# Seven half-size products for the output in four more chunks of two batches, with the output products a chunk later and the scores placed by slot

## The chip, the cores and the metric

The kernel runs on one core of a Trainium2 chip. The metric is the time on the device in microseconds (us), the median of three runs. TensorE (PE) multiplies matrices into PSUM, VectorE (DVE) and ScalarE (ACT) work on tiles elementwise, GpSimd (POOL) and SyncE (SP) mostly issue transfers here.

## The reference

Four batches of 5,824 tokens with 256 channels go through a channel attention, and then all tokens through a feed-forward network without a nonlinearity but one elementwise product.

```python
B, N, C = (4, 5824, 256);  d_ff = 1024

qn = q / (norm(q, axis=1) + 1e-06)        # norms over the tokens
kn = k / (norm(k, axis=1) + 1e-06)
s = kn.transpose(0, 2, 1) @ qn / tau      # 256 x 256 per batch
a = softmax(s, axis=-1)
x = (v @ a).reshape(B * N, C)

ab  = (x @ w1) * (x @ w2)                 # tokens x 1024
out = (ab @ w3) @ w_out                   # tokens x 256
```

The kernel multiplies `w3 @ w_out` once (`W_sb`, 1024 x 256) and folds the 256 x 256 attention matrix of each batch into `w1` and `w2` (`Wf`). What is left for each token is two products with `Wf`, one elementwise product and one product with `W_sb`.

## The kernel before

A batch has `NCH` = 12 chunks of tokens: 11 of 512 and a last one of 192. A chunk has `FT` = 8 **slots**, one for each 128 of the 1,024 features. A slot computes the tiles `a` and `b` on TensorE, copies `a` to SBUF on ScalarE, and multiplies the two on VectorE into `ab` (`abh` in the profile). The products of `ab` with `W_sb` are put on a list (`pend`) and come some slots later. The batches are b = 0 to 3 in the code; the text counts them as first to fourth.

```python
LAG = 2
def bank(tag):                                 # PSUM
    if tag == "out":
        return {"tag": "out", "bufs": 3}
    turns[0] += 1
    return {"tag": f"ab{turns[0] % 4}", "bufs": 1}

def emit_ab(b, c, j):
    n = chunk_cols(c)                          # 512, in the last chunk 192
    tiles = []
    for w in range(2):
        t = psum.tile([P, 512], F32, name=f"{'ab'[w]}_{b}_{c}_{j}", **bank("ab"))
        for ct in range(CT):                   # two matmuls each
            nc.tensor.matmul(
                t[:, :n], lhsT=Wf[b][:, ct, w, j * P : (j + 1) * P], rhs=rhs_of(b, c, ct),
                start=(ct == 0), stop=(ct == CT - 1),
            )
        tiles.append(t)
    a_sb = work.tile([P, 512], BF16, tag="a_sb", name=f"as_{b}_{c}_{j}", bufs=4)
    nc.scalar.copy(a_sb[:, :n], tiles[0][:, :n])
    # ... (last chunk: into "left")
        if j % 4 == 0:
            halves[j // 4] = in_pool.tile([P, 4, 512], BF16, tag="big", name=f"abh_{b}_{c}_{j}", bufs=BIG_BUFS)
        ab = halves[j // 4][:, j % 4, :]
        nc.vector.tensor_mul(ab, a_sb, tiles[1])
    slot[0] += 1
    if not seven(b, c):
        pend.append((slot[0] + LAG, 1, lambda only=None: emit_out(b, c, j, ab, only)))
    elif j == FT - 1:
        fns = seven_products(b, c, *halves)
        fns[0]()
        pend.extend((slot[0] + 1, 2, fn) for fn in fns[1:])
```

The **direct** way to the output, `emit_out`, makes four matmuls of 256 columns per slot, 32 per chunk, and copies the sums out at the end of the chunk:

```python
def emit_out(b, c, j, ab, only=None):
    # ...
        nc.tensor.matmul(
            tl[h][:, o, :], lhsT=lhsT, rhs=W_sb[:, j, :],           # 256 columns
            start=(j == 0 and o == 0), stop=(j == FT - 1 and (small or o == 1)), skip_group_check=True,
        )
    if j == FT - 1:
        # ...
            nc.scalar.copy(o[:, 0:2, :], tl[0])
            nc.vector.tensor_copy(o[:, 2:4, :], tl[1])
            nc.sync.dma_start(out=rows[:, 4 * c : 4 * c + 4, :], in_=o)
```

The **seven-product** way splits the product of a chunk, `ab` by `W_sb`, into blocks of two by two, and makes seven block products in place of eight, each of eight matmuls of 128 columns (56 per chunk). Sums of blocks of `ab` are made on VectorE, sums of blocks of `W_sb` once (`combine_weights`, in the second batch).

```python
def seven(b, c):
    return b == B - 1 and c < NCH - 2          # ten chunks of the fourth batch

    # in seven_products:
    def keep(r, d):  nc.scalar.copy(quarter(r, d), st["A"])
    def join(nm, r, d):  nc.vector.tensor_add(quarter(r, d), st[nm], quarter(r, d))
    def sum1():  nc.vector.tensor_add(s1, a21, a22)
    def p1():    nc.vector.tensor_sub(s2, s1, a11); product("A", a11, w1, True); keep(0, 0)   # o_sb taken here
    def p5():    nc.vector.tensor_sub(s3, a11, a21); product("C", s1, t1, True)
    def p6():    product("A", s2, t2); keep(0, 1)
    def p7():    nc.vector.tensor_sub(s4, a12, s2); product("A", s3, t3); keep(1, 1)
    def p2():    join("C", 1, 1); product("B", a12, w21, True)
    def p4():    join("B", 0, 0); product("A", a22, t4); keep(1, 0)
    def p3():    product("C", s4, w22); join("C", 0, 1)     # then the transfer out
    return [sum1, p1, p5, p6, p7, p2, p4, p3]
```

While batch b runs, the **scores** of batch b + 1 are made: 23 pairs of token rows, each in three units (`sq` of q with two matmuls, `sq` of k with two matmuls, and the sum of the squares on VectorE). They, the loads (`moves`) and what follows the scores stand on an agenda that runs by a clock, which adds up the kernel's own estimate of the TensorE time:

```python
    # score_units: one pair
    nc.scalar.activation(out=dst[:, :, part, :], in_=src[:, o : o + 2, :], func=AF.Square)   # parts 0, 1
    for ct in range(CT):
        nc.tensor.matmul(G[:, ct, :], lhsT=qt[:, i, ct * P : (ct + 1) * P], rhs=kt[:, i, :], ...)
    nc.vector.tensor_add(accs[n], accs[n], sqs[0])                                           # part 2

    # make_agenda, batches after the first
    t0, t1 = 16.0, 98.0
    for i, (cst, fn) in enumerate(units):
        at(t0 + (t1 - t0) * i / len(units), cst, fn)
    for cst, t, fn in soft:                    # norms, exponentials, folding into Wf
        at(t1 + 1.0 + t, cst, fn)

for b in range(B):
    make_agenda(b)
    for c in range(NCH):
        for j in range(FT):
            run_due()
            emit_ab(b, c, j)
            # ... up to size 2 of what is due on pend, run_due() after each
```

Of the kernel before, what the change touches and what calls it, by code (L numbers as in the profile page):

```python
# [17 lines left out]
LAG = 2  # L18
# [7 lines left out]
def kernel(  # L26
# [14 lines left out]
    B, N, C = q.shape  # L41
# [9 lines left out]
    FT = F // P  # L51
# [414 lines left out]
    comb = {}  # L466

    def seven(b, c):
        return b == B - 1 and c < NCH - 2

    def combine_weights(step):

# [100 lines left out]
    def emit_ab(b, c, j):  # L573
        n = chunk_cols(c)
# [11 lines that stand above are left out]
        if c == NCH - 1:  # L586
            if b % 2 == 0 and j == 0:
                lefts[b // 2] = work.tile([P, FT, 2, P + LEFT], BF16, tag="left", name=f"left_{b}", bufs=1)
            both = lefts[b // 2][:, j, b % 2, :]
            nc.vector.tensor_mul(both, a_sb[:, :n], tiles[1][:, :n])  # L590
            ab = both[:, :P] if b % 2 == 0 else both[:, LEFT:]
        else:
# [4 lines that stand above are left out]
        last_ab[0] = ab  # L597
        slot[0] += 1
        if not seven(b, c):
            pend.append((slot[0] + LAG, 1, lambda only=None: emit_out(b, c, j, ab, only)))  # L600
        elif j == FT - 1:
            fns = seven_products(b, c, *halves)
            fns[0]()
            pend.extend((slot[0] + 1, 2, fn) for fn in fns[1:])
        clock[0] += 4 * (n * MM_COL + MM_FIX)

    def emit_out(b, c, j, ab, only=None):

        small = c == NCH - 1
        if small:  # L610
            lhs = [ab[:, :P]]
            if b % 2 == 1:
                lhs.append(lefts[b // 2][:, j, :, :].rearrange("p b t -> p (b t)")[:, P : P + 2 * LEFT])
        else:
            lhs = [ab[:, i * P : (i + 1) * P] for i in range(4)]
        if j == 0:
            out_tiles[b, c] = [
                psum.tile([P, 2, D], F32, tag="out", name=f"o_{b}_{c}_{h}", bufs=3)
                for h in range(len(lhs) if small else 2)
            ]  # L620
        tl = out_tiles[b, c]
        for s, lhsT in reversed(list(enumerate(lhs))) if small else enumerate(lhs):
            if only is not None and s != only:
                continue
            h, o = (s, 0) if small else divmod(s, 2)
            nc.tensor.matmul(  # L626
                tl[h][:, o, :], lhsT=lhsT, rhs=W_sb[:, j, :],
                start=(j == 0 and o == 0), stop=(j == FT - 1 and (small or o == 1)),
                skip_group_check=True,
            )  # L630
        clock[0] += len(lhs) * (D * MM_COL + MM_FIX)
        if j == FT - 1:
            o = work.tile([P, 4, D], F32, tag="o_sb", name=f"osb_{b}_{c}", bufs=3)
            rows = out[b * N : b * N + NT * P, :].rearrange("(p i) c -> p i c", i=NT)
            if small:
                if b % 2 == 1 and only != 0:
                    o2 = work.tile([P, D], F32, tag="kr", name=f"oleft_{b}", bufs=1)
                    nc.vector.tensor_copy(o2, tl[1][:, 0, :])
                    for m in (b - 1, b):
                        k = (m - b + 1) * LEFT  # L640
                        nc.sync.dma_start(out=out[m * N + NT * P : (m + 1) * N, :], in_=o2[k : k + LEFT, :])
                if only != 1:
                    nc.scalar.copy(o[:, 0, :], tl[0][:, 0, :])
                    other = nc.scalar if b == B - 1 else nc.sync
                    other.dma_start(out=rows[:, NT - 1, :], in_=o[:, 0, :])
            else:
# [3 lines that stand above are left out]
            if only is None:  # L650
                del out_tiles[b, c]
# [114 lines left out]
        nc.gpsimd.partition_all_reduce(m, ones_f, P, ReduceOp.add)  # L766


    def make_agenda(b):
        agenda.clear()  # L770
        clock[0] = 0.0
        n = b + 1
        if b == 0:
            at(0.5, 0.87, soft0[5])
            for i in range(4):
                at((1.7, 2.6, 3.5, 3.9)[i], 0.43, soft0[7 + i])
            at(0.0, 0.0, load_library)
            at(4.6, 0.5, lambda: transpose_half_on_pe(0, 0, 1, False))
            at(7.0, 0.5, lambda: transpose_half_on_pe(0, 1, 0, True))
            at(8.0, 0.5, lambda: transpose_half_on_pe(0, 1, 1, False))  # L780
            at(15.0, 0.0, transpose_w3)
            at(15.0, 0.0, lambda: transpose_piece(0, 2))
            for jt in range(FT):
                at(27.5 + 1.2 * jt, 0.87, lambda jt=jt: w_unit(jt))
            moves = [("qk", 1, 0, 29.0), ("v", 0, 3, 30.0), ("v", 0, 4, 30.5), ("qk", 1, 1, 44.0), ("qk", 1, 2, 45.0)]
            moves += [("qk", 1, 3, 53.0), ("qk", 1, 4, 55.0), ("v", 0, 5, 61.0), ("qk", 1, 5, 73.0)]
            moves += [("v", 1, 0, 88.0), ("v", 1, 1, 98.0), ("v", 1, 2, 120.0), ("qk", 2, 0, 130.0)]
            t0, t1 = 54.0, 113.0
        else:
            moves = [("v", b, 3, 1.0), ("qk", n, 1, 10.0), ("qk", n, 2, 17.0), ("v", b, 4, 26.0), ("qk", n, 3, 38.0)]  # L790
            moves += [("v", b, 5, 46.0), ("qk", n, 4, 58.0), ("qk", n, 5, 66.0)]
            moves += [("v", n, 0, 76.0), ("v", n, 1, 86.0), ("v", n, 2, 96.0), ("qk", n + 1, 0, 108.0)]
            moves = [m for m in moves if m[1] < B]
            t0, t1 = 16.0, 98.0

        before = (0, 2) if b == 0 else None
        for nm, m, pi, t in moves:
            if before is not None and not (nm == "v" and before == (m, pi - 1) == (0, 3)):
                at(t, 0.0, lambda w=before: hold(vTs[w[0]][1][:1, 0, :1] if w[1] == NP_ - 1 else vTs[w[0]][0][:1, w[1] * PIECE, 0, :1]))
            at(t, 0.0, gate)  # L800
            if nm == "qk":
                at(t, 0.0, lambda m=m, pi=pi: load_qk(m, pi))
                before = None
            else:
                at(t, 0.0, lambda m=m, pi=pi: load_piece("v", m, pi))
                at(t + 4.0, 0.0, lambda m=m, pi=pi: transpose_piece(m, pi))
                before = (m, pi)
        if b == 1:
            for i in range(4):
                at(3.0 + 2.6 * i, 0.0, lambda i=i: combine_weights(i))  # L810
        if n == B:
            agenda.sort()
            return
        units = score_units(n)
        for i, (cst, fn) in enumerate(units):
            at(t0 + (t1 - t0) * i / len(units), cst, fn)
        soft = soft_units(n)
        for cst, t, fn in soft:
            at(t1 + 1.0 + t, cst, fn)
        agenda.sort()  # L820

    for b in range(B):
        make_agenda(b)
        for c in range(NCH):
            for j in range(FT):
                run_due()
                emit_ab(b, c, j)
                lag = 0
                if b == B - 1 and c >= NCH - 2:
                    lag = LAG_END if c == NCH - 1 else LAG + (LAG_END - LAG) * (j + 1) // FT  # L830
                room = 2
                while w_ready[0] and len(pend) > lag and pend[0][0] <= slot[0] and pend[0][1] <= room:
                    _, size, fn = pend.pop(0)
                    fn()
                    room -= size
                    run_due()
        run_due(1e9)
# [39 lines left out]
```

## Time and profile before

| | before |
|---|---|
| median of three runs | 566.84 us (566.59 to 566.93) |
| span of the profiled run | 564.8 us |
| granted TensorE clock | 1.0 |
| busy: DVE, ACT, POOL | 403.5 (71%), 348.7 (62%), 78.3 us (14%) |
| weight loads on TensorE (PEld) | 355.3 us (63%) |
| DMA packets | 77.50 MB, mean 137 GB/s |

The profile is of one execution. It lists busy time by engine, the chain of work that ended last, groups of instructions by source line (L579 are the products `a` and `b`, L626 the direct output products, L510 the seven products, L201 the score products, L596 the elementwise product, L585 the copy of `a`, L198 the squares, L210 the sum of squares), and the time of every instruction. For each stretch of the span the busy time of each engine can be read. Weight loads overlap the matmuls.

### The profile page before, as it was taken

The numbers are of one execution on the slowest core, as the hardware profiler recorded it, in microseconds if no ns is written. First come the engines' busy times: TensorE is split into PE (matmuls) and PEld (weight loads), VectorE is DVE, ScalarE is ACT, GpSimd is POOL, SyncE is SP. The second block draws the span as 40 slices with busy tenths as digits, with TensorE's granted clock in tenths as the row PEclk, the third lists the DMA queues.
The fourth block names the chain that finished last, engine by engine and source line by source line (L and its number), as shares of the span: only waits on it lengthen the run. The fifth ranks groups of instructions, "written<-read, shape, count | busy, mean of one in ns | idle before, by whom it ended". The sixth has DMA issues, their size and how long they took to land.

```text
span 564.8 us, 10684 instructions
## 1 busy us (share of the span) xinstructions
PE 553.4 (98%) x3988; PEld 355.3 (63%) x3995; DVE 403.5 (71%) x645; ACT 348.7 (62%) x659; POOL 78.3 (14%) x163
## 2 busy tenths in 40 slices
PE   7799999999999999999999999999999999999997
PEld 5764576776656666666656666666655666666665
DVE  1047645888967777888766567878876688888884
ACT  1047535777766577777665577777766666665663
POOL 4260013120120110120120010112020000100000
PEclk9999999999999999999999999999999999999999
DMA  9999989968455696685761586766650233440102
GB/s 214 211 181 209 171 175 230 226 169 198 112 150 113 112 215 148 110 158 146 151 152 43 133 180 157 137 132 122 158 152 38 67 93 79 98 102 38 75 39 95
DMA packets 75108, 77.50 MB, mean 137 GB/s; under 512 B 54192, under 2 KB 58800, under 8 KB 75056
## 3 DMA queue, kind: packets, MB, share of 16 engines
q0 software_dynamic: 15760, 38.93, 39.6%
q1 hardware_dynamic: 59008, 37.23, 22.5%
q10 hardware_dynamic: 288, 0.66, 0.4%
q8 instruction: 31, 0.51, 0.4%
q14 instruction: 21, 0.17, 0.1%
HBM read 78.91 MB, written 23.86 MB: 182 GB/s over the span
## 4 chain that ended last, share of the span: by engine, by line
PE 92%; DMA 5%; ACT 1%; DVE 1%; POOL 0%; issue 0%; DVEq 0%; ACTq 0%; POOLq 0%
PE b L579 28%; PE a L579 28%; PE o L626 22%; PE G L201 5%; DMA k<-in_k_dram 5%; PE prodA L510 3%; PE fold L370 2%; PE prodC L510 2%; PE w L752 1%; PE prodB L510 1%; ACT kr L292 0%; DVE Wf L379 0%; PE quarter L394 0%; POOL k L120 0%; POOL q L120 0%
## 5 line engine op out<-in xcount | busy, mean ns | idle before, releaser
L596 DVE TENSOR_TENSOR abh<-as,b 128x512 bf16<-128x512 bf16 x352 | 240.6, 685 | 116.1 <-ACT as L585 109.7
L585 ACT CAST as<-a 128x512 bf16<-128x512 f32 (+1 forms) x384 | 215.9, 562 | 146.1 <-PE a L579 94.7
L579 PEld LDWEIGHTS <-Wf 128*128 128x128 bf16 x1536 | 146.1, 98 | 103.8 <-issue 1.4
L579 PE MATMUL a<-vT,Wf 128*128 128x512 bf16 x704 | 209.4, 379 | 0.5 <-ACT Wf L403 0.4
L579 PE MATMUL b<-vT,Wf 128*128 128x512 bf16 x704 | 209.4, 379 | 0.0
L626 PE MATMUL o<-W_sb,abh 128*128 128x256 bf16 x1088 | 161.4, 273 | 0.0
L626 PEld LDWEIGHTS <-abh 128*128 128x128 bf16 x1088 | 106.3, 98 | 61.1 <-issue 0.2
L210 DVE TENSOR_TENSOR acc<-acc,sq 128x1024 f32<-128x1024 f32 x66 | 80.4, 1218 | 0.6 <-ACT sq L198 0.6
L201 PE MATMUL G<-k,q 128*128 128x256 bf16 x276 | 49.8, 273 | 0.0
L198 ACT ACTIVATE sq<-q 128x512 f32<-128x512 bf16 x66 | 41.8, 633 | 0.0
L198 ACT ACTIVATE sq<-k 128x512 f32<-128x512 bf16 x66 | 41.5, 629 | 0.0
L567 POOL COPY gate_t<-abh 1x1 bf16<-1x1 bf16 x39 | 10.5, 269 | 170.1 <-DVE abh L596 167.7
L201 PEld LDWEIGHTS <-q 128*128 128x128 bf16 x276 | 27.0, 98 | 3.1
L510 PEld LDWEIGHTS <-comb_S 128*128 128x128 bf16 x320 | 21.2, 98 | 9.4
L571 POOL COPY gate_t<-vT 1x1 bf16<-1x1 bf16 x16 | 2.9, 184 | 161.6 <-DMA vT<-v 161.6
L648 DVE COPY osb<-o 128x512 f32<-128x512 f32 x34 | 23.3, 684 | 0.9 <-PE o L626 0.9
L520 ACT COPY osb<-prodA 128x256 f32<-128x256 f32 x40 | 14.9, 372 | 11.7 <-PE prodA L510 11.7
L647 ACT COPY osb<-o 128x512 f32<-128x512 f32 x34 | 19.9, 586 | 3.5 <-PE o L626 2.1
L510 PEld LDWEIGHTS <-abh 128*128 128x128 bf16 x240 | 15.9, 98 | 7.1
L257 DVE TENSOR_TENSOR dk<-sqk,ident 128x256 f32<-128x256 f32 x1 | 0.4, 424 | 23.8 <-PE sqk L234 23.8
L377 ACT ACTIVATE Wf<-fold,rs 128x512 bf16<-128x512 f32 x15 | 10.3, 687 | 11.3 <-PE fold L370 8.1
L120 POOL DMA_DIRECT2D q<-in_q_dram x28 | 15.1, 541 | 12.7 <-DMA k<-in_k_dram 5.7
(116 smaller groups left out, 338.7 us busy)
## 6 DMA issues: line engine op xcount, KB each, us to landing
out_dram<-osb SPq DMA_DIRECT2D x44, 512.0 KB, 3.1
k<-in_k_dram POOLq DMA_DIRECT2D x19, 512.0 KB, 8.5
v<-in_v_dram POOLq DMA_DIRECT2D x19, 512.0 KB, 5.3
q<-in_q_dram POOLq DMA_DIRECT2D x18, 512.0 KB, 6.1
w_wout<-in_moe_w_dram POOLq DMA_DIRECT2D x1, 2048.0 KB, 23.0
k<-in_k_dram POOLq DMA_DIRECT2D x4, 320.0 KB, 8.2
v<-in_v_dram POOLq DMA_DIRECT2D x4, 320.0 KB, 5.0
q<-in_q_dram POOLq DMA_DIRECT2D x3, 320.0 KB, 4.2
```

What stands on the lines that cost most here:

```text
L120: nc.gpsimd.dma_start(out=pieces[nm, n, pi][:, lo:hi, :], in_=qk_main[nm, n][0][:, pi * PIECE + lo : pi * PIECE + hi, :])
L198: nc.scalar.activation(out=dst[:, :, part, :], in_=src[:, o : o + 2, :], func=AF.Square)
L201: nc.tensor.matmul(G[:, ct, :], lhsT=qt[:, i, ct * P : (ct + 1) * P], rhs=kt[:, i, :], start=(pr == 0 and part == 0 and ct == 0), stop=(pr ...
L210: nc.vector.tensor_add(accs[n], accs[n], sqs[0])
L510: nc.tensor.matmul(st[nm][:, i, :], lhsT=a[:, j, i * P : (i + 1) * P], rhs=w[j], start=(first and j == 0 and i == 0), stop=(j == 3), skip_ ...
L520: nc.scalar.copy(quarter(r, d), st["A"])
L579: nc.tensor.matmul(t[:, :n], lhsT=Wf[b][:, ct, w, j * P : (j + 1) * P], rhs=rhs_of(b, c, ct), start=(ct == 0), stop=(ct == CT - 1),)
L585: nc.scalar.copy(a_sb[:, :n], tiles[0][:, :n])
L596: nc.vector.tensor_mul(ab, a_sb, tiles[1])
L626: nc.tensor.matmul(tl[h][:, o, :], lhsT=lhsT, rhs=W_sb[:, j, :], start=(j == 0 and o == 0), stop=(j == FT - 1 and (small or o == 1)), skip ...
L647: nc.scalar.copy(o[:, 0:2, :], tl[0])
L648: nc.vector.tensor_copy(o[:, 2:4, :], tl[1])
```

## The change

It has four parts.

1. Four chunks each (0, 1, 4 and 7) of the second and third batch take the seven-product way too. It is for doing less work on TensorE.
2. In these two batches the direct output products come 8 slots after their `ab`, not 2. So the output products of one chunk lie in the slots of the next, whichever way they are made.
3. The score units of these batches are no longer placed by the clock but by slot, from slot 4 to 70 of the 96, with a weight for each slot: none in the first four slots after a chunk with seven products and in the last two of such a chunk, 0.4 in the next three, 1 elsewhere. It is for keeping VectorE free where the sums of blocks are made. What follows the scores starts at slot 71.
4. The load of the second pair of q and k pieces comes before that of the fourth v piece, since the scores start earlier.

```diff
     def seven(b, c):
-        return b == B - 1 and c < NCH - 2
+        return c < NCH - 2 if b == B - 1 else b > 0 and c in (0, 1, 4, 7)
+
+    def scores_of(b, s):
+
+        j = s % FT
+        after = s >= FT and seven(b, s // FT - 1)
+        if (after and j < 4) or (seven(b, s // FT) and j >= FT - 2):
+            return 0.0
+        return 0.4 if after and j < FT - 1 else 1.0
...
         if not seven(b, c):
-            pend.append((slot[0] + LAG, 1, lambda only=None: emit_out(b, c, j, ab, only)))
+            pend.append((slot[0] + (FT if 0 < b < B - 1 else LAG), 1, lambda only=None: emit_out(b, c, j, ab, only)))
...
+    SLOT0, SLOT1 = 4, 71
+    by_slot = []
+
+    def scores_due(slot_):
+
+        while by_slot and by_slot[0][0] <= slot_:
+            for cst, fn in by_slot.pop(0)[1]:
+                clock[0] += cst
+                fn()
...
-            moves = [("v", b, 3, 1.0), ("qk", n, 1, 10.0), ("qk", n, 2, 17.0), ("v", b, 4, 26.0), ("qk", n, 3, 38.0)]
+            moves = [("qk", n, 1, 1.0), ("v", b, 3, 8.0), ("qk", n, 2, 17.0), ("v", b, 4, 26.0), ("qk", n, 3, 38.0)]
...
-            t0, t1 = 16.0, 98.0
+            t0, t1 = None, None
...
+        if b > 0:
+            weights = [scores_of(b, s) for s in range(SLOT0, SLOT1)]
+            whole_ = sum(weights)
+            done = 0.0
+            for s, w in zip(range(SLOT0, SLOT1), weights):
+                first = -(-len(units) * done // whole_)
+                done += w
+                last = -(-len(units) * done // whole_) if s < SLOT1 - 1 else len(units)
+                by_slot.append((s, units[int(first) : int(last)]))
+
+            def chain():
+                for cst, t, fn in soft:
+                    at(clock[0] + 1.0 + t, cst, fn)
+                agenda.sort()
+
+            by_slot.append((SLOT1, [(0.0, chain)]))
+            agenda.sort()
+            return
...
                 run_due()
+                if b > 0:
+                    scores_due(c * FT + j)
                 emit_ab(b, c, j)
```

More of the change, by code (lines that the diff above doesn't have):

```diff
@@ L814, in make_agenda @@
         units = score_units(n)
+        soft = soft_units(n)
+        if b > 0:
[14 more added lines that the diff above has]
+            return
         for i, (cst, fn) in enumerate(units):
             at(t0 + (t1 - t0) * i / len(units), cst, fn)
-        soft = soft_units(n)
         for cst, t, fn in soft:
```

## The prediction

> **What bounds the kernel now.** I read the engines' busy times first, then the chain of work that ended last, then busy time by stretch. Columns of the first fence: engine, busy us, share of the span, instructions; then the chain's shares.
>
> ```profile
> PE 553.4 (98%) x3988; PEld 355.3 (63%) x3995; DVE 403.5 (71%) x645; ACT 348.7 (62%) x659; POOL 78.3 (14%) x163
> ...
> PE 92%; DMA 5%; ACT 1%; DVE 1%; POOL 0%; issue 0%; DVEq 0%; ACTq 0%; POOLq 0%
> ```
>
> TensorE is busy 98%, and 92% of the chain is its own work. A busy share is an average, so I looked at the second batch's scores (two stretches) and at a chunk of the fourth batch, which has the seven products already. Columns: stretch, length, then busy us of PE, PEld, DVE, ACT, POOL, clock, DMA share, GB/s.
>
> ```profile
> 247.00:257.00 10.00, 10.00 (x67) 6.28 (x65) 8.61 (x14) 7.34 (x14) 2.34 (x5) 1.00 0.84 172
> 267.00:277.00 10.00, 10.00 (x68) 6.46 (x67) 8.11 (x12) 7.50 (x14) 0.88 (x3) 1.00 0.71 164
> 463.30:473.30 10.00, 10.00 (x91) 6.22 (x89) 8.69 (x16) 6.13 (x13) 0.70 (x2) 1.00 0.13 52
> ```
>
> TensorE has no gap in any of them, at full clock. VectorE is at 81 to 87% and is next. So time is won only by fewer TensorE cycles, and lost as soon as VectorE or ScalarE can't hand back a PSUM bank in time. From the start of the second batch (first product at 180.40) to 440.55 TensorE is busy 259.94 of 260.15 us: there is no idle time to win in the two batches that change.
>
> **What the Trainium skill says.** "TensorE: Matmul & The Clock Gate", section "Wait — 56ns, not 53.3ns?", gives N/2.4 ns plus about 2.5 ns for a warm matmul of N columns: an estimate of 55.8 ns at 128 and 109.2 ns at 256. The trace agrees: eight seven-product matmuls take 0.45 us in the chain (56 ns each), four direct ones 0.44 us (109 ns). "VectorE: DVE Perf Modes", section "The perf-mode tier table (the rule you actually need)", lets a bf16 tensor_tensor in SBUF make two results per cycle, and one in fp32 or out of PSUM only one. The trace agrees: a block sum of 1,024 bf16 elements (L530) takes 684 ns, as long as the 512-element product out of PSUM (L596, 685 ns); 1,024 in fp32 (L210) take 1,218 ns. The first page, section "Architectural detail: the array is 16× 32×32, not 1× 128×128", calls the ACT and DVE queues strict FIFO: a long sum ahead of an `ab` product delays it. The trace agrees where it can be seen: at 225.39 a sum of squares (1.22 us) starts on VectorE and the next product starts at 226.52.
>
> **The change part by part.**
>
> *Fewer TensorE cycles.* The chain, in order of time (start, us, what), first in a direct stretch of the second batch, then around the border of two seven-product chunks:
>
> ```profile
> 286.15 0.43 PE a L579 x2
> 286.58 0.43 PE b L579 x2
> 287.01 0.44 PE o L626 x4
> 287.45 0.43 PE a L579 x2
> ```
>
> ```profile
> 453.29 0.45 PE prodA L510 x8
> ...
> 461.14 0.45 PE prodC L510 x8
> 461.59 0.43 PE a L579 x2
> 462.02 0.43 PE b L579 x2
> 462.45 0.43 PE a L579 x2
> 462.89 0.43 PE b L579 x2
> 463.32 0.45 PE prodA L510 x8
> ```
>
> A direct slot is 287.45 - 286.15 = 1.30 us, a chunk of eight 10.40 us. A seven-product chunk runs from one first product to the next, 463.32 - 453.29 = 10.03 us. The difference is 0.37 us; by the formula above it is 32 x 109.2 - 56 x 55.8 = 369 ns, the same. Two batches with four such chunks: 8 x 0.37 = **2.96 us** saved, all on the path.
>
> *More work on VectorE and ScalarE.* Groups by line (columns: line, engine, operation, tiles, shapes, count, busy us, mean ns, idle before and its releaser):
>
> ```profile
> L648 DVE COPY osb<-o 128x512 f32<-128x512 f32 x34 | 23.3, 684 | 0.9 <-PE o L626 0.9
> L520 ACT COPY osb<-prodA 128x256 f32<-128x256 f32 x40 | 14.9, 372 | 11.7 <-PE prodA L510 11.7
> L647 ACT COPY osb<-o 128x512 f32<-128x512 f32 x34 | 19.9, 586 | 3.5 <-PE o L626 2.1
> L523 DVE TENSOR_TENSOR osb<-prodC,osb 128x256 f32<-128x256 f32 x20 | 8.3, 416 | 0.0
> L530 DVE TENSOR_TENSOR comb_S<-comb_S,abh 128x1024 bf16<-128x1024 bf16 x10 | 6.8, 684 | 0.0
> ```
>
> Per chunk VectorE gets four block sums (about 2.74 us) and three joins (1.25) for one copy (0.68): +3.3 us, 26 us in all. ScalarE gets four copies of 0.372 for one of 0.586: +0.9 us, 7 us in all. Whether that lies beside TensorE's work depends on the densest places. Durations on VectorE overlap: in the fourth batch it starts 685 ns operations at 453.37, 453.98, 454.57, 455.17 and 455.77, one per 0.60 us, and the sum of squares above held it 1.13 us. I use these two pitches, and whole durations elsewhere.
>
> - Scores at full weight: the 36.4 weights share 69 units, 1.9 per slot, 0.63 of a pair. TensorE: 1.30 + 0.63 x 0.44 = 1.58 us. VectorE: 0.60 + 0.63 x 1.13 + an eighth of a copy = 1.39 us, 88%. ScalarE: 0.58 + 0.63 x 1.26 + an eighth of 0.59 = 1.45 us, 92%.
> - The chunk after a single seven-product chunk: weights of 2.2, so 1.4 pairs. VectorE: 8 x 0.60 + three block sums 1.80 + joins 1.25 + 1.4 x 1.13 = 9.4 us of TensorE's 10.03 + 1.4 x 0.44 = 10.65 us, 89%.
>
> So no chunk goes over TensorE's time, and the weights keep the sums of squares off the slots with block sums, where VectorE has 0.60 + 0.60 for a 1.31 us slot. Within a slot, `ab` may end about two slots after its `a` (four banks, two per slot), some 2.6 us, against about 1.4 us now. One or two queued operations fit.
>
> *The first chunk of the second batch* is the one place without this room. Slots 2 to 7 have no output products, so a slot is 0.87 us of TensorE and the room is about 1.7 us. Two steps of `combine_weights` (0.69 each), the first block sum and three squares on ScalarE (0.63 each, slots 4 and 5) come on top. I followed the queues slot by slot with the durations above and get one TensorE wait of 0.2 us at slots 6 to 8; I book **0.3 us** with the rest of such hiccups. The fourth batch's first chunk has such slots now, without extras, and TensorE isn't held (0.86 us a slot from 447.94 to 452.26).
>
> *The later output products* cost nothing by themselves: one slot's worth per slot still. They fill the short slots of the last chunk, where TensorE now loses some 0.2 us waiting for `left` (443.3): **-0.1 us** booked. *What follows the scores* starts at slot 71, by the kernel's clock at 99 to 100.5 against 99, and by the same clock the batch ends some 6 us after the last fold. No effect.
>
> *Loads.* The first pieces for the third batch's scores land at 178.3 (k issued 171.27, 7.0 us), before slot 4 at about 184. The tightest is the fourth pair: issued at 220.6 and 221.1 (agenda time 38, unchanged), landing after 4.9 and 6.8 us, at 228. The scores need it at slot 37: 37 x 0.87 + 14 products x 0.45 + 13 direct outputs x 0.44 + 12 pairs x 0.44 = 49.4 us after 180.4, at 229.8. Under 2 us of room; k loads took up to 8.8 us here. I book **0.2 us**.
>
> The sum: 566.84 - 2.96 + 0.3 - 0.1 + 0.2 = **564.3 us**, 0.45% less.
>
> **The rivals.**
>
> *VectorE or ScalarE becomes the bound in the dense stretches.* For: 88 to 92% by averages, sums of squares in two of three slots, strict queues; a copy or join next to two sums of squares makes a queue of over 2 us. Against: the fourth batch runs at 87% on VectorE without a TensorE gap. If each of the eight chunks lost 0.3 to 0.5 us, the gain would be gone: 566 to 568 us.
>
> *A wait for a load takes the saving.* For: scores start at slot 4, not at 16 us, and take the fourth pair at 50, not 59 us (16 + 82 x 36/69). Against: they then pause until slot 45, so one late landing costs once, at most 1 to 2 us per batch: 565 to 567 us.
>
> *The smaller matmuls are bound by weight loads.* 56 loads per chunk in place of 32. Against: the fourth batch shows 6.22 us of loads in 10 with TensorE gapless. It would make the saving zero; I hold it for excluded.
>
> **Range and chances.** The saving has a hard floor of 2.96 us, plus 0.2 of idle time: nothing below about 563.5 us. Above, I allow one rival at half strength: 565.9. Faster by over 2% would need 11 us less, and slower by 2% 11 us more; neither has a mechanism, so nearly all falls within 2%.
>
> **What would show it.** Right: L510 at 56 x 18 = 1,008 matmuls, L626 with 256 fewer, PE busy about 3 us lower, and the second and third batch each about 1.5 us shorter, from first product to first product. For the rival of the engines: TensorE waits for `abh` or `as` between the second batch's slots 24 and 64, and below 10.00 busy in 10 us stretches there. For the load: a wait of L201 for a DMA at slot 37. Most doubtful are the first 20 us of the second batch and my evenness of queues in the dense slots.

## The result, and the profile after

The changed kernel takes **564.46 us** (563.97 to 565.21, six runs), the kernel before 566.85 us in the same comparison; the ratio is 0.9958, with a 95% interval of 0.9945 to 0.9971. That is 2.4 us less; 564.3 was predicted.

The profile of the changed kernel has the same picture as before: TensorE is 98% busy, and its own work is 90% of the chain.

```profile
PE 552.9 (98%) x4180; PEld 356.8 (63%) x4187; DVE 424.9 (76%) x693; ACT 355.8 (63%) x683; POOL 79.8 (14%) x163
...
PE 90%; DMA 7%; POOL 1%; DVE 1%; ACT 1%; issue 0%; POOLq 0%
```

TensorE's busy time is only 0.5 us less over the whole run. Two things hide in that number. From the second batch on it is 3.01 us less (380.01 before, 377.00 after). Before that, where the change touches nothing, it is 2.5 us more, 2.4 of them in the first 20 us, when the first loads come in; this cost nothing, as the first product `a` starts at 37.16 us (37.18 before). The second, third and fourth batch (columns as in the prediction), first before, then after:

```profile
180.40:312.99 132.59, 132.43 (x864) 83.54 (x862) 99.73 (x151) 89.97 (x169) 19.32 (x40) 1.00 0.63 136
312.99:445.13 132.14, 131.91 (x859) 83.19 (x858) 97.57 (x147) 89.07 (x167) 17.08 (x36) 1.00 0.58 129
445.13:564.80 119.67, 115.67 (x996) 73.13 (x993) 97.01 (x170) 70.26 (x140) 3.04 (x9) 1.00 0.28 77
```

```profile
181.34:311.25 129.91, 129.66 (x948) 82.37 (x947) 109.66 (x175) 92.88 (x181) 20.00 (x40) 1.00 0.63 135
311.25:442.37 131.12, 131.02 (x961) 83.70 (x960) 108.47 (x172) 92.59 (x179) 17.58 (x36) 1.00 0.60 130
442.37:562.70 120.33, 116.32 (x1002) 73.73 (x999) 97.55 (x170) 70.83 (x140) 3.37 (x9) 1.00 0.27 80
```

Three stretches of 10 us in the second batch (same columns):

```profile
190.00:200.00 10.00, 10.00 (x90) 6.36 (x89) 9.96 (x18) 6.73 (x14) 1.04 (x2) 1.00 0.64 122
210.00:220.00 10.00, 10.00 (x68) 6.47 (x67) 9.79 (x14) 8.09 (x15) 1.16 (x1) 1.00 0.74 157
250.00:260.00 10.00, 10.00 (x70) 6.65 (x69) 9.33 (x12) 8.52 (x17) 2.66 (x6) 1.00 0.47 76
```

TensorE (the third number) has no gap. VectorE (the fifth) was at 81 to 87% in the stretches of the prediction and is at 93 to 100% here. The chain over the first seven-product chunk of the second batch:

```profile
190.46 0.45 PE prodA L518 x8
...
200.71 0.45 PE prodA L518 x8
```

From one first product to the next it is 10.25 us, of which 0.22 us are two score products: 10.03 us, the length that the fourth batch showed before. L518 (L510 before) has 1,008 weight loads, L634 (L626) 256 fewer than before. The profile names one wait of TensorE in the second and third batch, of 0.15 us:

```profile
PE b L587 <- DVE abh L604: 0.2, 1, 0.2
...
189.87 0.59 PE L587 MATMUL b<-vT,Wf 128*128 128x512 bf16 x2 [0.15 <-DVE abh L604]
```

Before, it named one of 0.18 us, in the short slots of the third batch's last chunk, and this one is gone:

```profile
443.47 0.32 PE L579 MATMUL b<-vTt,Wf 128*128 128x192 bf16 x2 [0.18 <-DVE left L590]
```

The lengths of the stages in the profiled runs, from one batch's first full-width product `a` to the next one's, show where the time went. The last column works the difference out from the 0.37 us per chunk, the two waits and what moved from one batch to the next:

| stage | before | after | difference | worked out |
|---|---|---|---|---|
| second batch | 132.59 | 129.91 | -2.68 | -1.48 for four chunks, -1.31 moved out, +0.15 wait = -2.64 |
| third batch | 132.14 | 131.12 | -1.02 | -1.48, +1.31 in, -0.65 out, -0.18 wait = -1.00 |
| fourth batch, to the end | 119.67 | 120.33 | +0.66 | +0.65 moved in |
| sum | 384.40 | 381.36 | **-3.04** | -2.99 |

"Moved" are the output products of a last chunk that now come a batch later. They are those of six slots (those of the last two crossed the border before, too), with two matmuls of 109 ns each between the second and third batch, and with one between the third and fourth. The spans of the two profiled runs differ by only 2.1 us, since the first batch, which the change doesn't touch, took 0.9 us more in this run. It waited for a load of v:

```profile
45.68 0.62 PE L143 MATMUL tr_I-615_616<-ident_b,v 128*128 128x128 bf16 x8 [0.77 <-DMA v<-in_v_dram]
```

In the thirteen profiled runs of this document the first batch took 143.2 to 144.7 us, though only e10 changes anything in it. So up to 1.5 us of difference between two single executions can come from there, and the lengths from the second batch on, though of one execution each, are the better measure of an edit.

### The profile page after: what moved, and what is told of

It is laid out like the page before. It is cut to its first block, busy times and chain, and to the rows that moved or that the text cites. A ratio compares the mean times of both kernels' runs of the same rounds, so it can differ in the third digit from the quotient of the medians.

```text
span 562.7 us, 11089 instructions
## 1 busy us (share of the span) xinstructions
PE 552.9 (98%) x4180; PEld 356.8 (63%) x4187; DVE 424.9 (76%) x693; ACT 355.8 (63%) x683; POOL 79.8 (14%) x163
## 4 chain that ended last, share of the span: by engine, by line
PE 90%; DMA 7%; POOL 1%; DVE 1%; ACT 1%; issue 0%; POOLq 0%
PE b L587 27%; PE a L587 27%; PE o L634 17%; PE prodA L518 6%; PE G L201 5%; DMA k<-in_k_dram 5%; PE prodC L518 3%; DMA v<-in_v_dram 2%; PE fold L370 2%; PE prodB L518 1%; PE w L760 1%; POOL w L729 0%; DVE abh L604 0%; ACT as L593 0%; POOL w L728 0%
## 5 line engine op out<-in xcount | busy, mean ns | idle before, releaser
L587 PEld LDWEIGHTS <-Wf 128*128 128x128 bf16 x1536 | 144.4, 98 | 104.1 <-issue 1.7
L634 PE MATMUL o<-W_sb,abh 128*128 128x256 bf16 x832 | 123.0, 273 | 0.0
L634 PEld LDWEIGHTS <-abh 128*128 128x128 bf16 x832 | 81.0, 98 | 41.7 <-issue 0.2
L210 DVE TENSOR_TENSOR acc<-acc,sq 128x1024 f32<-128x1024 f32 x66 | 80.4, 1219 | 0.6 <-ACT sq L198 0.6
L518 PEld LDWEIGHTS <-comb_S 128*128 128x128 bf16 x576 | 38.2, 98 | 17.0 <-DVE comb_S L534 0.2
L528 ACT COPY osb<-prodA 128x256 f32<-128x256 f32 x72 | 26.8, 373 | 21.3 <-PE prodA L518 21.3
L518 PEld LDWEIGHTS <-abh 128*128 128x128 bf16 x432 | 28.7, 98 | 12.7
L579 POOL COPY gate_t<-vT 1x1 bf16<-1x1 bf16 x16 | 4.4, 277 | 174.0 <-DMA vT<-v 174.0
L518 PE MATMUL prodA<-comb_T,comb_S 128*128 128x128 bf16 x288 | 22.0, 219 | 0.0
L656 DVE COPY osb<-o 128x512 f32<-128x512 f32 x26 | 17.8, 686 | 0.9 <-PE o L634 0.9
L598 DVE TENSOR_TENSOR left<-as,b 128x192 bf16<-128x192 bf16 x32 | 11.3, 353 | 9.5 <-ACT as L593 7.6
L655 ACT COPY osb<-o 128x512 f32<-128x512 f32 x26 | 15.2, 586 | 3.2 <-PE o L634 2.1
```

What stands on the lines that cost most here:

```text
L518: nc.tensor.matmul(st[nm][:, i, :], lhsT=a[:, j, i * P : (i + 1) * P], rhs=w[j], start=(first and j == 0 and i == 0), stop=(j == 3), skip_ ...
L587: nc.tensor.matmul(t[:, :n], lhsT=Wf[b][:, ct, w, j * P : (j + 1) * P], rhs=rhs_of(b, c, ct), start=(ct == 0), stop=(ct == CT - 1),)
L634: nc.tensor.matmul(tl[h][:, o, :], lhsT=lhsT, rhs=W_sb[:, j, :], start=(j == 0 and o == 0), stop=(j == FT - 1 and (small or o == 1)), skip ...
```

## The experiments

Two theories stood. **A**: the saving is TensorE work, 0.37 us per chunk, and the other parts only keep its queues fed, with room to spare. **B**: the queues have no room, and the placing of the other engines' work decides. The kernels are variants of the changed kernel unless stated. Each ratio is to the kernel before in the same comparison, where its median was 566.66 to 566.89 us. The lengths in the last two columns are from the profiled runs; the last column is from the second batch's first product `a` to the end.

| run | time, us | ratio to before (95%) | second, third batch | from the second batch on |
|---|---|---|---|---|
| before | 566.85 | 1 | 132.59, 132.14 | 384.40 |
| changed kernel | 564.46 | 0.9958 (0.9945-0.9971) | 129.91, 131.12 | 381.36 |
| e1 seven products alone | 568.10 | 1.0026 (1.0016-1.0037) | 133.57, 132.69 | 385.94 |
| e2 seven products and late outputs | 566.48 | 0.9995 (0.9986-1.0004) | 131.40, 132.34 | 384.05 |
| e3 the rest without seven products | 567.71 | 1.0022 (1.0012-1.0033) | 131.89, 133.19 | 385.39 |
| e4 all but late outputs | 569.96 | 1.0054 (1.0039-1.0069) | 133.96, 133.30 | 386.97 |
| e5 seven products in chunks 8 and 9 too | 573.56 | 1.0109 (1.0090-1.0129) | 135.00, 136.23 | 391.96 |
| e6 load 4 us later | 572.88 | 1.0108 (1.0088-1.0129) | 135.18, 133.69 | 389.16 |
| e7 folds later | 565.34 | 0.9979 (0.9969-0.9990) | 130.44, 131.66 | 382.47 |
| e8 as e3, folds earlier | 568.56 | 1.0034 (1.0021-1.0048) | 132.23, 133.52 | 386.11 |
| e9 seven products in chunk 9 too | 567.65 | 1.0013 (1.0005-1.0022) | 131.57, 132.78 | 384.66 |
| e10 combining in the first batch | 564.19 | 0.9951 (0.9935-0.9968) | 129.60, 131.12 | 381.10 |
| e11 one more reduction on GpSimd | 567.49 | 1.0016 (1.0008-1.0024) | 131.51, 132.95 | 384.77 |

### One part without the others (e1 to e4)

**e1**, of the four parts only the first:

```diff
-            pend.append((slot[0] + (FT if 0 < b < B - 1 else LAG), 1, ...))
+            pend.append((slot[0] + LAG, 1, ...))
-        if b > 0:                     # scores by slot
+        if False:                     # scores by the clock, 16.0 to 98.0; loads in the old order
```

> The seven products in chunks 0, 1, 4, 7 of the second and third batch alone; direct outputs two slots late, scores by the clock, loads in the old order. Theory (the saving is TensorE work, the other parts only keep its queues fed): TensorE still does 2.96 us less, but waits for abh or as in the slots of 0.87 us that have no output products and in the crowded slots after them, 1 to 3 us in the two batches: 565.0 to 567.0 us. Rival (the other parts are without effect): no waits in the two batches, 564.0 to 564.7 us.

It came out slower than the kernel before, 1.1 us over what theory A allowed. **e2** has late outputs again, with the scores by the clock and the loads in the old order:

> As the one before, and the direct outputs eight slots late; scores still by the clock. Theory: even slots of about 1.3 us leave room for one or two queued operations, so squares on top of block sums cost under 0.5 us of TensorE waits: 564.0 to 564.9 us. Rival (VectorE needs the squares placed by slot): waits of 1 us or more after the chunks with seven products, 565.3 us or more.

The rival was right: the late outputs win 1.6 us by the medians, and the squares by slot another 2.0 (1.9 and 2.7 us by the lengths from the second batch on). The second step brings the new order of loads as well, but neither kernel's trace shows TensorE waiting for a load in these batches. The timeline of e2 shows one of the costs. A sum of squares (L210) falls between the second and third block sum of chunk 4, and the weight load for the product that needs the third sum (L543) waits for it:

```profile
235.96 0.68 DVE L538 TENSOR_TENSOR comb_S<-comb_S,abh 128x1024 bf16<-128x1024 bf16 x1
...
236.56 1.22 DVE L210 TENSOR_TENSOR acc<-acc,sq 128x1024 f32<-128x1024 f32 x1
...
238.30 0.68 DVE L543 TENSOR_TENSOR comb_S<-abh 128x1024 bf16<-128x1024 bf16 x1
...
239.03 0.45 PEld L518 LDWEIGHTS <-comb_S 128*128 128x128 bf16 x8 [0.50 <-DVE comb_S L543]
```

**e4** has everything but the late outputs:

> The whole change, but direct outputs two slots late as before. Theory: the slots of a chunk with seven products have no output products, so they last 0.87 us, or 1.15 with the scores, against 1.31 us of VectorE; TensorE waits for abh some 0.2 to 0.6 us in each such chunk, 1 to 4 us in all: 565.3 to 568 us. Rival (the lag is idle): 564.0 to 564.8 us.

The direction was A's, the size was not: 5.5 us over the changed kernel, of which TensorE's named waits are 3.4 us. Two slots late, the direct outputs are done early in a seven-product chunk, and its later slots have only `a`, `b` and the scores. The weights put full scores just there:

```profile
231.80 1.22 DVE L210 TENSOR_TENSOR acc<-acc,sq 128x1024 f32<-128x1024 f32 x1
...
232.94 1.27 DVE L604 TENSOR_TENSOR abh<-as,b 128x512 bf16<-128x512 bf16 x2
...
233.67 0.59 PE L587 MATMUL b<-vT,Wf 128*128 128x512 bf16 x2 [0.48 <-DVE abh L604]
```

So scores placed by slot cost 1.9 us without late outputs (e1 to e4; 1.0 by the lengths) and win 2.0 us with them (e2 to the changed kernel; 2.7 by the lengths). The parts don't add up; they fit each other.

**e3** is the counterpart, the schedule without the seven products:

```diff
     def seven(b, c):
-        return c < NCH - 2 if b == B - 1 else b > 0 and c in (0, 1, 4, 7)
+        return b == B - 1 and c < NCH - 2      # scores_of keeps (0, 1, 4, 7)
```

> Late outputs, scores by slot with the same weights and the new order of loads, but direct products in all chunks of the second and third batch. Theory: the same TensorE work as before, less the 0.2 us that it waited for left: 566.3 to 566.9 us. Rival (a part of the gain comes from the new order, not from the seven products): 566.0 us or less.

The schedule alone costs 1.0 us, by the medians and by the lengths; neither expectation had that. On top of it the seven products bring 3.3 us by the medians and 4.0 us by the lengths: the 2.96 us of TensorE work, and two waits of 0.57 us that the changed kernel doesn't have. There is one in each batch (the second batch's here), where the end of a chunk, the last fold and the short slots of the last chunk meet:

```profile
305.51 0.68 DVE L659 COPY osb<-o 128x512 f32<-128x512 f32 x1
...
306.11 0.74 DVE L379 TENSOR_SCALAR Wf<-fold,rs 128x512 bf16<-128x512 f32 x1
...
306.90 0.33 PE L590 MATMUL b<-vTt,Wf 128*128 128x192 bf16 x2 [0.57 <-DVE Wf L379]
```

### Where the folds lie (e7, e8)

Is that meeting the loss of e3? **e8** moves all that follows the scores 0.44 us of the kernel's clock earlier (`clock[0] + 0.56 + t` in place of `1.0`), **e7** moves it as far later in the changed kernel (`1.44`).

> The rest of the change alone (direct products in all chunks of the second and third batch), with what follows the scores 0.44 us earlier. Theory: the last fold moves back by a slot, off the copies at the end of the chunk, and the 1.0 us over the kernel before goes: 566.4 to 567.0 us. Rival (the loss lies in the first chunk or in the dense squares): 567.5 us or more.

> The whole change, with all that follows the scores 0.44 us of the kernel's clock later, which moves some folds by one slot, against the last chunk. Theory (in the run of the rest alone the last fold meets the copies at the end of a chunk and the short slots of the last chunk, 0.57 us of waiting per batch): TensorE waits 0.4 to 0.6 us more per batch, 565.0 to 565.8 us. Rival (where the folds lie is indifferent): 564.2 to 564.8 us.

In e8 the wait at the last fold is gone, and the kernel is slower still: now the scaling of the scores and the exponentials meet the copies at a chunk's end (chain at 293 to 297), a wait of 0.2 us shows at `a`, and the two batches are 0.3 us longer each than in e3. The theory that one move repairs e3 fell. e7 had the size that was expected, +0.5 us per batch, but at another place: the time is lost in the slot of the first folds (from 296.09, 2.45 us for 1.95 us of products), not at the last, and the profile names no wait for it. So a move of 0.44 us on the kernel's clock changed a batch by 0.3 to 0.5 us, and which meeting it would be was not foreseen either time.

### The room of the load (e6)

```diff
-("v", b, 4, 26.0), ("qk", n, 3, 38.0)]
+("v", b, 4, 26.0), ("qk", n, 3, 42.0)]
```

> The whole change, with the fourth pair of q and k pieces asked for 4 us later (agenda time 42 in place of 38). In the changed kernel k was asked for at 221.72, took 8.3 us, landed at 230.0, and the score product that needs it started at 230.98. Theory (the room is about 1 us): the product waits some 2.5 to 3.5 us in the second batch and 1 to 3 us in the third: 567.5 to 571 us. Rival (the time to landing adapts, or the scores have more room than read): 564 to 565 us.

The product waited as theory A said, 3.4 and 2.4 us, so the changed kernel's room is really about 1 us. But the time rose by 8.4 us (7.8 from the second batch on in the profiled run), more than the waits:

```profile
PE G L201 <- DMA k<-in_k_dram: 5.8, 2, 3.4
```

```profile
230.00:234.00 4.00, 0.57 (x6) 0.38 (x4) 1.82 (x2) 0.63 (x1) 0.00 (x0) 1.00 1.06 205
234.00:238.00 4.00, 4.00 (x17) 2.00 (x15) 1.05 (x2) 1.17 (x2) 0.00 (x0) 0.59 0.45 97
```

The first line of the second fence is the wait in the second batch. In the next the granted clock is 0.59 on average: after the idle stretch TensorE ran slow for some 4 us, an estimated 4 x 0.41 = 1.6 us lost on top. "TensorE: Matmul & The Clock Gate", section "What's actually happening", in the Trainium skill says that an idle window of some 3.4 us drops the clock to half; the trace agrees in the second batch (wait 3.4 us), and in the third (2.4 us) the clock stayed at 1.00.

### More chunks (e5, e9) and a reduction (e11)

**e5**: `c in (0, 1, 4, 7, 8, 9)`. The block sums of chunks 8 and 9 come after the scores.

> The whole change, with chunks 8 and 9 of the second and third batch on seven products too, where the scores are done. Theory (0.37 us of TensorE work per chunk wherever VectorE has room): four more chunks, 1.48 us less than the changed kernel, 562.6 to 563.4 us. Rival (block sums and joins meet what follows the scores, the norms and the folds, and TensorE waits): 564.2 us or more.

It lost 9 us, in place of winning 1.5. The second batch's timeline:

```profile
284.56 3.23 POOL L271 PARTITION_ALL_REDUCE tot<-acc  x1 [2.26 <-DVE acc L269]
...
284.97 2.37 DVE L543 TENSOR_TENSOR comb_S<-abh 128x1024 bf16<-128x1024 bf16 x1
...
287.40 0.62 PE L518 MATMUL prodA<-comb_T,comb_S 128*128 128x128 bf16 x8 [1.59 <-DVE comb_S L543]
```

A block sum that takes 0.68 us elsewhere took 2.37 us while GpSimd reduced the sums of squares over the partitions. **e11** tests that by itself: the changed kernel with one more such reduction at slot 9, its result unused.

```diff
+                if 0 < b < B - 1 and c == 1 and j == 1:
+                    extra_reduce(b + 1)       # gpsimd.partition_all_reduce of 512 fp32 columns
```

> The whole change, with one more reduction over the partitions on GpSimd (512 fp32 columns of the sums of squares, its result unused) at slot 9 of the second and of the third batch, where chunk 0's block sums are made. Theory (a VectorE operation with two operands in SBUF can't start while GpSimd runs the reduction): one block sum there takes 2 to 3 us in place of 0.69, the products that need it wait, and TensorE loses 1 to 2.5 us per batch: 566.5 to 569 us. Rival (the long block sum of the other run had another cause): block sums stay at 0.69 us and the time at 564.2 to 564.8 us.

```profile
193.43 3.18 POOL L780 PARTITION_ALL_REDUCE extra<-acc  x1
193.68 2.48 DVE L543 TENSOR_TENSOR comb_S<-abh 128x1024 bf16<-128x1024 bf16 x1
...
196.22 0.62 PE L518 MATMUL prodA<-comb_T,comb_S 128*128 128x128 bf16 x8 [1.34 <-DVE comb_S L543]
```

The theory's numbers held: one block sum per batch took 2.48 and 2.82 us, and the batches grew by 1.6 and 1.8 us. Each of the four slow block sums in e5 and e11 ended about 0.45 us before its reduction did. "SBUF — State Buffer", section "Who interferes with whom", in the Trainium skill says that a VectorE instruction with two SBUF inputs contends with a GpSimd instruction that reads SBUF, and that one with at most one such input, outside the two-port modes, doesn't. The trace agrees: in the changed kernel `ab`, with one operand in PSUM, keeps its 0.69 us during the reduction. That the second SBUF operand makes the difference is the skill's reason. The two operations also differ in their number of columns and in the results per cycle, and no run here separates these.

```profile
283.49 3.18 POOL L271 PARTITION_ALL_REDUCE tot<-acc  x1
...
284.40 0.69 DVE L604 TENSOR_TENSOR abh<-as,b 128x512 bf16<-128x512 bf16 x1 [0.61 <-ACT as L593]
```

**e9** keeps chunk 9 and leaves out chunk 8, whose block sums met the reduction.

> The whole change, with chunk 9 alone added to the seven-product chunks of the second and third batch. In the run with chunks 8 and 9 one block sum took 2.37 us while GpSimd ran the reduction over the partitions, and TensorE waited for it. Theory (that meeting was most of the loss; chunk 9's block sums come after the reduction): the 0.74 us of TensorE work is saved, less some 0.3 us of waits where scale and exponentials lie: 563.6 to 564.5 us. Rival (any block sum after slot 71 costs more than it brings): 565 us or more.

The rival was right: every block sum takes 0.69 us again, and still 3.2 us are lost against the changed kernel. The longest wait that the trace names, 0.47 us in each batch, goes through ScalarE's queue. The first exponential waits on ScalarE for its scaled scores, which stand on VectorE behind a block sum and a copy; the copy of `a` stands behind the exponential:

```profile
295.18 0.51 ACT L331 ACTIVATE e<-s,r 128x256 bf16<-128x256 f32 x1 [1.65 <-DVE s L326]
295.60 0.56 ACT L593 CAST as<-a 128x512 bf16<-128x512 f32 x1
...
296.21 0.59 PE L587 MATMUL a<-vT,Wf 128*128 128x512 bf16 x2 [0.47 <-ACT as L593]
```

In each batch 0.3 us more are a wait for folded weights, and the rest of the loss is not named. e5's trace has the same kind of wait beside the reduction's. The second exponential there waits for its scaled scores, and the copies of `a` and of a block product stand behind it:

```profile
298.74 0.51 ACT L331 ACTIVATE e<-s,r 128x256 bf16<-128x256 f32 x1 [1.69 <-DVE s L326]
...
300.05 1.01 PE L518 MATMUL prodA<-comb_T,comb_S 128*128 128x128 bf16 x8 [1.63 <-ACT osb L528]
```

Over both batches TensorE's named waits in e5 are 3.2 us for the block sums in the reduction and 3.3 us for such copies. So the reduction is only a part of e5's loss, not most of it.

### The one wait that was left (e10)

```diff
-        if b == 1:
+        if b == 0:
             for i in range(4):
-                at(3.0 + 2.6 * i, 0.0, lambda i=i: combine_weights(i))
+                at(40.0 + 2.6 * i, 0.0, lambda i=i: combine_weights(i))
```

> The whole change, with the four steps that combine the blocks of W moved from the start of the second batch to the first batch, at 40.0 to 47.8 of its clock. Theory (they are what makes TensorE wait 0.15 to 0.25 us in the short slots of the second batch's first chunk): that wait goes and nothing else changes: 564.0 to 564.5 us, and no PE wait for abh at the eighth slot of the second batch. Rival (the first batch has no room for them): 564.8 us or more.

It held: the wait of 0.15 us is gone (it lay in slot 8 counted from 0, the first of chunk 1), the second batch is 0.31 us shorter, the third as in the changed kernel. At 564.19 us it is the lowest time of all; the intervals of e10 and the changed kernel overlap, so that it is faster is shown by the trace alone.

## Why the prediction was right

- **0.37 us per chunk, 2.96 us**: right. The new chunk has the length read off the fourth batch, TensorE's busy time from the second batch on fell by 3.01 us, and the stages account for 3.04 us with 2.99 worked out.
- **564.3 us, with 564.46 measured**: so close partly by luck. From the second batch on the kernel saved 3.04 us, where the prediction's terms give 2.96 - 0.3 + 0.1 - 0.2 = 2.56. Most of the booked losses did not come, and a wait in the first batch that has nothing to do with the change, 0.9 us in the profiled run, made up for it.
- **The first chunk of the second batch, 0.3 us booked**: right in place and kind, one wait of 0.15 us at slot 8; e10 shows that `combine_weights` causes it.
- **The wait for `left`, -0.1 us booked**: right. The 0.18 us in the third batch are gone.
- **A load, 0.2 us booked**: not incurred. The k piece took 8.3 us, not 6.8, and landed at 230.0; the product that needs it started at 230.98, 49.6 us after the batch's first product (49.4 was worked out, though the terms as given add up to 49.5). The room was named, and e6 shows it is that small.
- **"No chunk goes over TensorE's time"**: right for this placing. But the 88 and 89% for VectorE are averages over a slot and a chunk, and the densest 10 us are 93 to 100% busy. VectorE's busy time rose by 21.4 us (26 were worked out, from whole durations, which overlap), ScalarE's by 7.1 (7). "One or two queued operations fit" holds only as long as they don't meet in the same slots: e1, e2 and e4 have the same TensorE work in these batches and show waits of up to 0.5 us at such meetings.
- **"The later output products cost nothing by themselves"**: wrong as a statement on the part. Without them the change loses 5.5 us (e4), and with the schedule but without seven products there is a meeting with the folds of 0.57 us per batch (e3). The sum came out right because in the changed kernel these things happen to cancel or to miss each other.
- **"The second and third batch each about 1.5 us shorter"**: wrong, -2.7 and -1.0, with +0.7 in the fourth. The prediction forgot that late outputs carry products over the batch's end.
- **"What follows the scores: no effect"**: right for the changed kernel, but nothing in the working secured it: e7, e8 and e9 show 0.3 to 1.7 us per batch for one slot or one chunk there.

Open is what each single meeting in e1, e2 and e8 costs. In e1 the named waits are 2.0 us, while the second and third batch are 4.5 us longer than the work alone gives. The profile records the start of a matmul and works out its end from a model, so waiting can lie inside what it shows as busy. e1 fits this: from the second batch on it runs the same matmuls as the changed kernel, but TensorE is busy for 379.5 us there, and for 377.0 us in the changed kernel (e1 below: its waits for `abh`, all in the second and third batch, then the stretch from the second batch on):

```profile
PE b L587 <- DVE abh L604: 2.0, 7, 0.5
...
180.86:566.80 385.94, 379.49 (x2906) 239.47 (x2905) 316.04 (x515) 255.55 (x498) 41.43 (x85) 1.00 0.50 115
```

## What to carry to other kernels

Work removed from the engine that sets the end is worth its full time only if the work put on the others arrives at an even rate: here 2.96 us less of TensorE work became -2.4 us in the changed kernel, +1.4 us in e1 and +3.2 us in e4, by placing alone. Average shares are not enough to tell. Follow each queue slot by slot, also across engines: in e5 and e9 a short operation that waited held up the copies behind it, and then TensorE. Before adding VectorE work with two operands in SBUF, look for a reduction on GpSimd at the same time.

## What was not expected of the hardware

- A VectorE block sum with two operands in SBUF took 2.37 to 2.82 us in place of 0.69 us beside a GpSimd reduction of 3.2 us (e5, e11), and ended only about 0.45 us before it; products with an operand in PSUM kept their 0.69 us.
- A wait of TensorE of 3.4 us cost an estimated 1.6 us more, in a clock of 0.59 over the next 4 us; after one of 2.4 us the clock stayed at 1.00 (e6).
